# A tuned two-layer transformer kernel: VectorE's score tiles as TensorE tasks of their own, small PV bursts, and four elementwise steps on GpSimd

## The chip, the cores and the metric

The kernel runs on one core of a Trainium2 chip. The metric is the device time of one execution in microseconds (us), lower is better. All times here are of fast executions of one core, unless a line says otherwise. With one core there is no second die to compare with, so an execution counts as slow when it is more than 1.5% above the fastest of the same kernel.

## The reference

Four residual blocks over one sequence of 2048 tokens with 512 features: attention, feed-forward, attention, feed-forward.

```python
def _A_ref(x, wqkv, wo):                       # 32 heads of 16
    qkv = (x @ wqkv).reshape(B, S, 3, 32, 16)  # then transposed
    scores = einsum("bhqd,bhkd->bhqk", q, k) * 16 ** -0.5
    o = einsum("bhqk,bhkd->bhqd", softmax(scores), v)
    return o.transpose(0, 2, 1, 3).reshape(B, S, D) @ wo
def _B_ref(x, w1, b1, w2, b2):                 # 512 -> 1376 -> 512
    h = gelu(einsum("bsd,df->bsf", layernorm(x), w1) + b1)
    return einsum("bsf,fd->bsd", h, w2) + b2
x = x + _A_ref(layernorm(x), A_wqkv, A_wo);  x = x + _B_ref(layernorm(x), ...)
x = x + _A_ref(layernorm(x), A_wqkv, A_wo);  x = x + _B_ref(layernorm(x), ...)
```

The scores of both attention layers are 2 x 32 x 2048 x 2048 numbers, which is 4096 tiles of 128x512. Every one needs an exponential.

## The kernel before

The program is laid out when it is built. A list scheduler keeps a clock of its own, gives every instruction a planned duration, and emits for each engine a fixed order. **The plan is not used when the kernel runs, but the order it led to is.** In the tuple of an instruction, the number after the reads and writes is the planned duration in us.

```python
class Sched:                                   # [cut]
    def best(self, e):                         # what engine e takes next
        f = self.P.free[e]
        lim = f + self.LOOK[e]
        for t in self.pend[e]:
            r = self.task_ready(t)             # by planned durations
            if r <= lim: ...                   # ready: the lowest (prio, seq)
            else: ...                          # else: the one ready first
```

Score tiles go two ways. ScalarE takes two or three tiles at a time through its exponential. VectorE takes single tiles: an integer add on the fp32 score gives the bits of an approximate bf16 exponential, three more integer adds give shifted copies, and TensorE multiplies all four with V and three scaled copies of V, so that the errors average out. The matmuls of exponentials with V are called PV; several of them in a row are a burst. The work between two transfers of an attention accumulator out of PSUM (TensorE's output memory) is a segment; there are 88. GpSimd makes the scaled copies of V (`vs`).

```python
            dts = []                           # VectorE's tiles that ride along
            while self.wide and len(grp) + len(dts) < 4:
                d = self.take_d([rows already used in this run])   # [cut]
                if d is None: break
                dts.append(d)
            ops = []
            for (sg, j), b in zip(grp, banks):
                ops.append(self.score(sg, j, b))
            for sg, j, b, bt, w in dts:        # one TensorE task for all of them
                ops.append(self.score(sg, j, b))
            ...
            yield Task("pe", 0.0, ops)
    # [cut] the scaled copies of V, three for each group of n key blocks
    yield Task("pool", 0.8, [I(lambda e, k=k: e.tensor_scalar(out=self.vs[:, q, k - 1, i:i + n, :], in0=src, scalar1=WSHIFT[k], scalar2=None, op0=ALU.mult),
                               [("V", hg, kb) for kb in kbs], [("vs", q, i + k2) for k2 in range(n)], 0.15 + 0.06 * n, ...) for k in (1, 2, 3)])
    # [cut] the norm apply, and at the end of a segment: division, transpose
    Task("dve", prio, [I(... e.tensor_scalar(out=dst, in0=x, scalar1=mean, scalar2=rs, op0=ALU.subtract, op1=ALU.mult), ..., 0.39)])
    yield Task("dve", 1.2, [I(... e.tensor_tensor(out=ob[:, :, 0:16], in0=T[:, :, 0:16], in1=rv..., op=ALU.mult), [RA, ("rv", a)], [("ob", o)], 0.15 + 0.26 * W / 512)])
    yield Task("dve", 1.2, [I(... e.transpose(self.OT[:, hg, 0:W], self.ob[:, o, 0:W]), [("ob", o)], [("OT", hg)], 0.17 + 0.53 * W / 512)])
```

A score matmul has 32 rows, so a head takes one of four groups of TensorE's rows (`tile_position=(32 * hp, 0)`), and a run of up to four score matmuls can use four different groups. Gaps that the plan leaves on TensorE are filled with matmuls by zeros (`zw`), which are meant to keep its clock up.

Of the kernel before, what the change touches and what calls it, by code (L numbers as in the profile page):

```python
# [14 lines left out]
ALU = mybir.AluOpType  # L15
# [417 lines left out]
DLANE = 5  # L433
DBATCH = 2
# [11 lines left out]
PV_LEAST = 0.75  # L446


class Builder:
# [330 lines left out]
    def ln_apply(self, tt, slot, i, dst, dres, prio):  # L780
        c = 4 * slot + i
        return Task("dve", prio, [I(lambda e: e.tensor_scalar(out=dst, in0=self.xres[:, tt, :], scalar1=self.mv[:, c, 0:1], scalar2=self.rs[:, c:c + 1], op0=ALU.subtract, op1=ALU.mult),
                                    [("x", tt), ("mv", c), ("rs", slot)], [dres], 0.39)])
# [16 lines left out]
    def job_qkv_tile(self, L, tt, slot, i, left, prio, what):  # L800
# [9 lines left out]
        yield self.ln_apply(tt, slot, i, xnr, RX, prio)  # L810
# [83 lines left out]
        if not start:  # L894
            yield Task("dve", prio, [I(lambda e: e.tensor_tensor(out=sq, in0=v4, in1=v4, op=ALU.mult), [("qk", qs, k) for k in range(k0, k1)], SR, 0.12 + 0.0085 * N)])
# [65 lines left out]
    def job_qt(self, sg, s):  # L961
        L, part, hg = sg["L"], sg["part"], sg["hg"]
        k = (L // 2) * 2 + part
        q = yield ("get", "qt")
        sg["qslot"] = q
        yield ("keys", [("scl", L, part)])
        W = sg["W"]
        src, RS = (self.psbf(self.q0bank)[:, 0:512], ("ps", self.q0bank)) if s is None else (self.qraw[:, s, 0:W], ("qraw", s))
        yield Task("dve", 0.4, [I(lambda e: e.tensor_scalar(out=self.QT[:, q, 0:W], in0=src, scalar1=self.scl[:, k, hg:hg + 1], scalar2=self.qbias[:, 0:1], op0=ALU.mult, op1=ALU.add),
                                  [RS, ("scl", k), ("qbias",)], [("qt", q)], 0.39)])  # L970
        if s is None:
            self.S_.release("mb", self.q0bank)
        else:
            self.S_.release("qraw", s)
        self.S_.mark(("qt", sg["i"]))
        if sg["dks"] and not (L == 1 and sg["nparts"] == 2 and part == 0):
            step = 1 if L == 1 and sg["qc"] == 0 else len(sg["dks"])
            for i in range(0, len(sg["dks"]), step):
                self.S_.spawn(self.job_vs(sg, i, sg["dks"][i:i + step]), 0.8)
# [66 lines left out]
    def flow_scores(self):  # L1046
# [11 lines left out]
        while True:  # L1058
# [43 lines left out]
            for sg, j, b, bt, w in dts:  # L1102
                ops.append(self.score(sg, j, b))
# [9 lines left out]
            for d in dts:  # L1113
                self.d_load(d)
# [68 lines left out]

    def close_batch(self):
        bt = self.batch
        self.batch = None
        bt["closed"] = True
        if bt["loaded"] == len(bt["tiles"]):
            self.S_.spawn(self.job_d(bt), 2.0)
# [9 lines left out]
    def d_loaded(self, bt, w, b):  # L1199
        self.dload -= 1  # L1200
        if b == DLANE:
            self.lane_busy = False
        else:
            self.S_.release("mb", b)
        self.d_ready(bt, 0, bt["unit"], [w])
# [34 lines left out]
    def try_pv(self):  # L1240
        S_ = self.S_
        while True:
# [16 lines left out]
            if value(r) < PV_LEAST and not self.starved and len(near) < sg["n"] - sg["sub"]:  # L1259
                return  # L1260
# [23 lines left out]
            S_.submit(Task("pe", 1.0, ops), cb=lambda sg=sg, pick=pick: self.pv_done(sg, pick))  # L1284

# [11 lines left out]
    def job_segend(self, sg):  # L1297
# [44 lines left out]
        yield Task("dve", 1.2, [I(lambda e: e.tensor_tensor(out=ob[:, :, 0:16], in0=T[:, :, 0:16], in1=rv.unsqueeze(2).broadcast_to([128, nb, 16]), op=ALU.mult), [RA, ("rv", a)], [("ob", o)], 0.15 + 0.26 * W / 512)])  # L1342
# [39 lines left out]
    def job_yt(self, L, tt, slot, i, left, pr):  # L1382
        S_ = self.S_
        xr = yield ("get", "xn")
        yield self.ln_apply(tt, slot, i, self.xn[:, xr, :], ("xn", xr), pr - 1)
# [140 lines left out]
    def build(self):  # L1526
# [4 lines left out]
        self.pv_first = False  # L1531
        self.starved = False
# [78 lines left out]
```

## Time and profile before

| | before |
|---|---|
| median of 4 runs | 1710.28 us (1708.60 to 1712.83) |
| span of the profiled run | 1708.6 us |
| busy: TensorE, VectorE, ScalarE, GpSimd | 93%, 80%, 94%, 22% |
| mean granted TensorE clock | 0.983 |
| exponentials on ScalarE, tiles on VectorE | 1348, 758 |

The prediction below shows the main lines of this profile. Three more views are needed later. In all lines PE is TensorE's matmuls, PEld its weight loads, DVE VectorE, ACT ScalarE, POOL GpSimd and SP SyncE. The first is from the page's costliest groups (line, engine, operation, shapes, count; busy us and mean ns; idle before it and the releaser): GpSimd's copies of V. With half of its time idle before them, they look harmless.

```profile
L986 POOL TENSOR_SCALAR vs<-V 128x340 bf16<-128x340 bf16 (+3 forms) x312 | 255.7, 826 | 859.7 <-PE ps L1278 833.1
```

The second is the page's 40 slices of the run, each digit the busy share of one slice in tenths; the last line is the granted clock.

```profile
ACT  4878999999999999999999999999999999999996
POOL 4045522102211121101212133411011101132220
PEclk9989999999999999999899999999999999999999
```

The third is the timeline: start, duration, engine, line, operation, and how many. Four score matmuls on four row groups take 0.40 us together.

```profile
508.09 0.40 PE L1127 MATMUL ps<-QT,KT 32*128 32x512 bf16 x4
```

### The profile page before, as it was taken

How to read it: one execution, taken by the hardware profiler on the slowest of the kernel's cores; microseconds unless marked ns; L12 is line 12 of the kernel's file. 1: busy time of each engine (PE TensorE's matmuls, PEld its weight loads, DVE VectorE, ACT ScalarE, POOL GpSimd, SP SyncE). 2: the span in 40 equal slices, each digit the busy share in tenths (PEclk: the TensorE clock that was granted, in tenths of full speed). 3: DMA queues.
4: the chain of work that ended last, by engine and by line, in shares of the span. 5: the costliest groups of instructions: out<-in, count | busy, mean ns of one | idle time of the engine just before them, and what ended most of it. 6: DMA issues, size and time to landing. Idle time of an engine off the chain costs nothing.

```text
span 1708.6 us, 46394 instructions
## 1 busy us (share of the span) xinstructions
PE 1585.4 (93%) x19711; PEld 568.6 (33%) x19711; DVE 1374.4 (80%) x3011; ACT 1609.6 (94%) x1426; POOL 378.5 (22%) x640
## 2 busy tenths in 40 slices
PE   8988999999999999999999998999999999999998
PEld 5222333233223223332223333323232233344444
DVE  6878998859876798768878799886888869887783
ACT  4878999999999999999999999999999999999996
POOL 4045522102211121101212133411011101132220
PEclk9989999999999999999899999999999999999999
DMA  6552000112101120112532230000000100010000
GB/s 167 104 103 69 26 12 8 47 43 59 33 17 41 40 73 14 29 28 69 117 54 54 56 87 18 17 20 11 14 8 8 20 15 5 5 21 7 19 10 14
DMA packets 181259, 66.70 MB, mean 39 GB/s; under 512 B 160859, under 2 KB 175424, under 8 KB 181056
## 3 DMA queue, kind: packets, MB, share of 16 engines
q1 hardware_dynamic: 181056, 63.75, 16.6%
q8 instruction: 158, 2.59, 0.6%
q14 instruction: 45, 0.37, 0.1%
HBM read 19.96 MB, written 15.30 MB: 21 GB/s over the span
## 4 chain that ended last, share of the span: by engine, by line
PE 47%; ACT 40%; DVE 8%; POOL 2%; issue 2%; DMA 1%; SPq 0%; DVEq 0%; POOLq 0%
ACT PT L1110 37%; PE ps L1127 15%; PE ps L1278 13%; PE ps L1035 4%; PE ps L841 4%; PE ps L1397 4%; DVE dp L1195 3%; PE ps L1364 3%; PE ps L1435 3%; ACT h L1427 2%; DVE dp L1223 2%; POOL vs L986 1%; DVE accT L1304 1%; PE ps L1038 1%; ACT L1110 1%
## 5 line engine op out<-in xcount | busy, mean ns | idle before, releaser
L1110 ACT ACTIVATE PT<-ps 128x1536 bf16<-128x1536 f32 (+1 forms) x1348 | 1534.3, 1262 | 67.0 <-PE ps L1127 61.3
L1127 PE MATMUL ps<-QT,KT 32*128 32x512 bf16 (+1 forms) x4608 | 604.2, 363 | 108.5 <-ACT PT L1110 43.8
L1195 DVE TENSOR_SCALAR dp<-ps 128x512 uint16<-128x512 f32 x758 | 510.2, 682 | 208.4 <-PE ps L1127 200.7
L1278 PE MATMUL ps<-PT,V 128*17 128x512 bf16 (+1 forms) x3751 | 469.7, 363 | 0.4 <-DVE accT L1304 0.4
L1223 DVE TENSOR_SCALAR dp<-dp 128x1024 uint16<-128x1024 uint16 (+1 forms) x1170 | 443.2, 422 | 12.7 <-PE ps L1278 8.2
L986 POOL TENSOR_SCALAR vs<-V 128x340 bf16<-128x340 bf16 (+3 forms) x312 | 255.7, 826 | 859.7 <-PE ps L1278 833.1
L1278 PE MATMUL ps<-dp,vs 128*17 128x512 bf16 (+1 forms) x2571 | 397.3, 359 | 0.0
L1127 PEld LDWEIGHTS ps<-QT,KT 32*128 32x128 bf16 x4608 | 163.4, 91 | 637.8 <-issue 173.3
L1035 PE MATMUL ps<-wqkv,zw 128*32 128x256 bf16 x6152 | 241.5, 280 | 1.1 <-DVE accT L1304 1.1
L1278 PE MATMUL ps<-dp,V 128*17 128x512 bf16 (+1 forms) x857 | 201.4, 364 | 3.0 <-DVE accT L1304 2.9
L1035 PEld LDWEIGHTS ps<-wqkv,zw 128*32 128x32 bf16 x6152 | 144.5, 97 | 93.3 <-issue 76.0
L1278 PEld LDWEIGHTS ps<-PT,V 128*17 128x17 bf16 x3751 | 114.7, 88 | 91.1 <-issue 73.7
L1278 PEld LDWEIGHTS ps<-dp,vs 128*17 128x17 bf16 x2571 | 101.9, 89 | 85.3 <-issue 71.4
L1397 PE MATMUL ps<-yT,wf 128*128 128x512 bf16 (+3 forms) x396 | 98.5, 359 | 0.5 <-DVE h L1421 0.3
L841 PE MATMUL ps<-wqkv,xnT 128*128 128x512 bf16 x336 | 94.2, 389 | 2.9 <-DVE dp L862 2.1
L1304 DVE STREAM_TRANSPOSE accT<-ps 128x512 f32<-128x512 f32 (+1 forms) x88 | 58.3, 662 | 24.4 <-PE ps L1278 22.9
L1421 DVE TENSOR_SCALAR h<-ps,b1c 128x512 bf16<-128x512 f32 (+2 forms) x88 | 62.0, 705 | 13.9 <-PE ps L1397 13.5
L1364 PE MATMUL ps<-wo,OT 128*128 128x512 bf16 x240 | 67.4, 383 | 0.2
L1278 PEld LDWEIGHTS ps<-dp,V 128*17 128x17 bf16 x857 | 48.9, 88 | 38.4 <-issue 24.3
L906 POOL TENSOR_TENSOR qt<-n,qy 128x32 f32<-128x32 f32 x32 | 11.1, 347 | 160.1 <-DVE qy L902 159.6
L1344 DVE STREAM_TRANSPOSE OT<-ob 128x512 bf16<-128x512 bf16 (+1 forms) x72 | 46.0, 640 | 0.2
L1397 PEld LDWEIGHTS ps<-yT,wf 128*128 128x128 bf16 (+1 forms) x396 | 29.5, 99 | 46.5 <-issue 18.6
(154 smaller groups left out, 820.1 us busy)
## 6 DMA issues: line engine op xcount, KB each, us to landing
wf<-in_B_w_dram SPq DMA_DIRECT2D x90, 128.0 KB, 2.8
q_scr<-qk SPq DMA_DIRECT2D x22, 256.0 KB, 2.1
k_scr<-qk SPq DMA_DIRECT2D x12, 256.0 KB, 2.0
out_dram<-xres SPq DMA_DIRECT2D x16, 128.0 KB, 1.7
v_scr<-vst SPq DMA_DIRECT2D x12, 136.0 KB, 2.0
V<-v_scr SPq DMA_DIRECT2D x8, 204.0 KB, 4.5
wqkv<-in_A_wqkv_dram SPq DMA_DIRECT2D x3, 512.0 KB, 3.9
q_scr<-h SPq DMA_DIRECT2D x6, 256.0 KB, 2.1
```

Of the source, the lines that this page charges most:

```text
L841: yield Task("pe", prio, [I(lambda e, c=c: e.matmul(self.ps[:, b, :], lhsT=xnT[:, c, :], rhs=self.wqkv[:, c, which * 512:which * 512 + 512 ...
L986: yield Task("pool", 0.8, [I(lambda e, k=k: e.tensor_scalar(out=self.vs[:, q, k - 1, i:i + n, :], in0=src, scalar1=WSHIFT[k], scalar2=None ...
L1035: P.op("pe", lambda e, p=p: e.matmul(self.ps[p:p + 32, b, 0:w], lhsT=self.zw[:, 0:32], rhs=rhs[:, 0:w], start=st, stop=st, skip_group_chec ...
L1110: S_.submit(Task("act", 1e-5 * gi, [I(lambda e, pt=pt, n=n, b0=b0: e.activation(out=self.PT[:, pt:pt + n, :], in_=self.ps[:, b0:b0 + n, :] ...
L1127: return [I(lambda e, kb=kb, i=i: e.matmul(self.ps[:, b, i * W:(i + 1) * W], lhsT=self.KT[32 * hp:32 * hp + 32, hg, kb * 128:(kb + 1) * 12 ...
L1195: self.S_.submit(Task("dve", 0.0, [I(lambda e: e.tensor_scalar(out=self.dp[:, u, w * 512:(w + 1) * 512], in0=self.ps[:, b, :], scalar1=BIT ...
L1223: yield Task("dve", pr, [I(lambda e, k=k, v=v: e.tensor_scalar(out=self.dp[:, v, 0:N], in0=self.dp[:, u, 0:N], scalar1=float(SHIFT[k]), sc ...
L1278: ops.append((i, I(lambda e, hp=hp, v=v, ap=ap[:, i * W:(i + 1) * W], first=first and i == 0, W=W: e.matmul(self.ps[32 * hp:32 * hp + 17, ...
L1304: yield Task("dve", 0.3, [I(lambda e: e.transpose(self.accT[:, a, 0:W], self.ps[:, ACCB, 0:W]), [("ps", ACCB)], [RA], 0.15 + 0.53 * W / 512)])
L1364: yield Task("pe", pr, [I(lambda e, hg=hg, i=i, b=b: e.matmul(self.ps[:, b, :], lhsT=self.OT[:, hg, i * 128:(i + 1) * 128], rhs=self.wo[:, ...
L1397: yield Task("pe", pr, [I(lambda e, c=c: e.matmul(self.ps[0:M, b, off:off + W], lhsT=self.w1(fc, c), rhs=self.yT[:, c, 0:W], start=(c == 0 ...
L1421: S_.submit(Task("dve", pr - 0.7, [I(lambda e, fc=fc, M=M, b=b: e.tensor_scalar(out=hv[0:M, fc * W:(fc + 1) * W], in0=self.ps[0:M, b, 0:W] ...
```

## The change

The intent is to give ScalarE, the bound, fewer score tiles. VectorE is to take more of them, and for that it is relieved of four kinds of work that go to the idle GpSimd. TensorE's idle time is to be used for small PV bursts instead of zeros. There are two parts.

*Scheduling*: VectorE's tiles become TensorE tasks of their own, one more is started when VectorE is about to run dry (`d_solo`), and PV bursts that are too small to be worth it are taken when TensorE would idle for 0.4 us.

*Moves*: four kinds of work go to GpSimd: norm apply, (x - mean) * rs; Q scaling, one multiply and add on Q; squares, for the norms of Q and K; and the division of a segment's output by its sum of exponentials.

```diff
+D_IDLE = 1.0
+D_PRIO = 0.5
+PV_IDLE = 0.4
     def ln_apply(self, tt, slot, i, dst, dres, prio, eng="dve"):      # called with "pool", but for the start
-        return Task("dve", prio, [I(lambda e: e.tensor_scalar(... op0=ALU.subtract, op1=ALU.mult), [...], [dres], 0.39)])
+        return Task(eng, prio, [I(lambda e: e.tensor_scalar(... op0=ALU.subtract, op1=ALU.mult), [...], [dres], 0.39 if eng == "dve" else 1.55)])
         # squares
-            yield Task("dve", prio, [I(... in0=v4, in1=v4, op=ALU.mult ..., 0.12 + 0.0085 * N)])
+            yield Task("pool", prio, [I(... in0=v4, in1=v4, op=ALU.mult ..., 0.2 + 0.035 * N)])
         # Q scaling
-        yield Task("dve", 0.4, [I(lambda e: e.tensor_scalar(out=self.QT[:, q, 0:W], ... op0=ALU.mult, op1=ALU.add), ..., 0.39)])
+        eng = "dve" if s is None or W < 512 else "pool"
+        yield Task(eng, 0.4, [I(lambda e: e.tensor_scalar(out=self.QT[:, q, 0:W], ... op0=ALU.mult, op1=ALU.add), ..., 0.39 if eng == "dve" else 1.55)])
         # scores
-            for sg, j, b, bt, w in dts:
-                ops.append(self.score(sg, j, b))
+            for d in dts:
+                S_.submit(Task("pe", -0.5, self.score(d[0], d[1], d[2])), cb=lambda d=d: self.d_load(d))
+    def d_solo(self):
+        if not self.wide or self.P.free["dve"] - S_.now + sum(pending VectorE work) > D_IDLE:
+            return
+        d = self.take_d([])
+        if d is not None:
+            S_.submit(Task("pe", D_PRIO, self.score(d[0], d[1], d[2])), cb=lambda: self.d_load(d))
         # PV
             if value(r) < PV_LEAST and not self.starved and len(near) < sg["n"] - sg["sub"]:
-                return
+                t = self.P.drain + PV_IDLE
+                if S_.now < t or self.pv_out:
+                    ...                        # look again at t
+                    return
         # division
-        yield Task("dve", 1.2, [I(... op=ALU.mult), [RA, ("rv", a)], [("ob", o)], 0.15 + 0.26 * W / 512)])
+        yield Task("pool", 0.6, [I(... op=ALU.mult), [RA, ("rv", a)], [("ob", o)], 0.2 + 0.55 * W / 512)])
```

(Cuts are marked with dots; the arithmetic of the moved instructions is unchanged.)

## The prediction

> **What bounds the kernel now.** I read the page first: busy shares, the 40 slices, the chain.
>
> ```profile
> PE 1585.4 (93%) x19711; PEld 568.6 (33%) x19711; DVE 1374.4 (80%) x3011; ACT 1609.6 (94%) x1426; POOL 378.5 (22%) x640
> ...
> PE 47%; ACT 40%; DVE 8%; POOL 2%; issue 2%; DMA 1%; SPq 0%; DVEq 0%; POOLq 0%
> ```
>
> Two engines stand at 93 and 94%, so the shares alone do not decide. The costliest groups do:
>
> ```profile
> L1110 ACT ACTIVATE PT<-ps 128x1536 bf16<-128x1536 f32 (+1 forms) x1348 | 1534.3, 1262 | 67.0 <-PE ps L1127 61.3
> L1127 PE MATMUL ps<-QT,KT 32*128 32x512 bf16 (+1 forms) x4608 | 604.2, 363 | 108.5 <-ACT PT L1110 43.8
> L1195 DVE TENSOR_SCALAR dp<-ps 128x512 uint16<-128x512 f32 x758 | 510.2, 682 | 208.4 <-PE ps L1127 200.7
> L1223 DVE TENSOR_SCALAR dp<-dp 128x1024 uint16<-128x1024 uint16 (+1 forms) x1170 | 443.2, 422 | 12.7 <-PE ps L1278 8.2
> L1035 PE MATMUL ps<-wqkv,zw 128*32 128x256 bf16 x6152 | 241.5, 280 | 1.1 <-DVE accT L1304 1.1
> ```
>
> The columns are line, engine, operation, shapes, count; then busy us and mean ns; then idle before and its releaser. 6152 of TensorE's matmuls multiply by `zw`, a tile of zeros: filler that keeps the clock up, 241.5 us in which TensorE looks busy and makes nothing. ScalarE has no filler. It waited only 67.0 us before its 1348 exponentials. The table of windows confirms it in the middle of the run (PE, PEld, DVE, ACT, POOL busy of 100 us):
>
> ```profile
> 500.00:600.00 100.00, 93.40 (x1153) 32.75 (x1153) 73.15 (x156) 97.69 (x83) 15.00 (x16) 1.00 0.19 42
> 1400.00:1500.00 100.00, 92.63 (x1430) 34.07 (x1431) 90.12 (x198) 99.40 (x88) 16.79 (x15) 1.00 0.02 5
> ```
>
> So **ScalarE is the bound** from about 32 us (first exponential) to 1686 us (last), and the kernel gets shorter by taking score tiles from it. There are 4096 tiles of 128x512; VectorE has 758 of them, ScalarE the other 3338. TensorE is a close second bound, since it runs in order and feeds both.
>
> Last, the largest single stall of ScalarE after the start, in the order of time:
>
> ```profile
> 103.72 3.95 SPq L817 DMA_TRANSPOSE xnT<-xn  x2
> ...
> 108.29 0.41 DVE L782 TENSOR_SCALAR xn<-xres,mv,rs 128x512 bf16<-128x512 bf16 x1 [7.16 <-DMA xnT<-xn]
> ...
> 109.74 1.03 PE L1127 MATMUL ps<-QT,KT 32*128 32x512 bf16 x4 [6.94 <-DVE dp L1195]
> ...
> 110.87 1.45 ACT L1110 ACTIVATE PT<-ps 128x1536 bf16<-128x1536 f32 x1 [6.23 <-PE ps L1127]
> ```
>
> A norm apply waits on VectorE for a buffer that a late DMA frees; a VectorE score tile stands behind it, TensorE behind that, ScalarE behind that: 6.23 us lost.
>
> **What the Trainium skill says.** SBUF — State Buffer, section "Who interferes with whom": VectorE in a two-port mode and GpSimd share a port pair under an exclusive lock, and the second to start is blocked. The trace agrees in direction, with less than whole blocking on average: the 1024-column integer copies of L1223 took 417 ns (902 that met no GpSimd instruction), 520 ns (83 that began during one), at most 953 ns. The PSUM reads of L1195 took 674 to 685 ns either way. GPSIMD Engine Reference, section "Key points": for elementwise work VectorE is about twice as fast. Here it is worse: 340 columns took GpSimd 1089 ns and 68 took 427, which is 2.43 ns a column, so 512 columns are about 1.51 us (my estimate) against 0.41 to 0.45 us on VectorE. TensorEngine Tiling (Array Packing), section "Key Properties": changing the tiling mode drains TensorE. The trace fits: between score matmuls (row tiles) and PV matmuls (column tiles) its weight loads show gaps of 0.23 us put down to issue, and a PV burst of 8 takes 0.60 us from start to the next scores. TensorE: Matmul & The Clock Gate, section "What's actually happening": idle TensorE falls to half clock. Here the granted clock was 0.983 on average, so what filler removal can do to it is open.
>
> **The change part by part.** The schedule is made when the program is built, so I counted the instructions of both built programs; only counts are used, no planned times.
>
> 1. *More tiles on VectorE.* 852 instead of 758, so ScalarE has 94 fewer. Its exponentials fall from 1348 to 1310. One costs 1534.3 / 1348 = 1.138 us of engine time (the means of 1262 overlap), so 38 x 1.138 = **43 us off the bound**. The gain is spread over the run: cut into 16 equal parts by score tiles, every part has fewer ScalarE tiles than before, by 1 to 15.
>
> 2. *VectorE's bill.* Removed: Q scaling 71 x 0.445 = 31 us, norm apply 70 x 0.41 = 27 (busy), squares about 21, divisions 29; together 108. Added: 94 tiles at 510.2 / 758 = 0.673, 63 us; 153 copies of 1024 columns at 0.387 (427.7 / 1104) less 24 of 512 at 0.26, 53 us. Sum +8 us. Lock: GpSimd will be busy about twice the share, so I take some 340 instead of 156 copies meeting it, at about 80 ns each: +15. VectorE comes to about 1374 + 8 + 15 = 1397 us, 84% of a shorter span. It had 334 us idle, of which 200.7 waiting for score tiles. **Not the bound.**
>
> 3. *GpSimd's bill.* Q scaling 71 x 1.51 = 107; norm apply 70 x 1.51 = 106; squares 16 of 1024 elements and 24 of 512, at an assumed 2.4 ns an element, 69; divisions 56 x 0.72 + 16 x 0.45 = 47 (like its 256-element tensor operations at 649 to 749 ns). Sum 329, so 378 + 329 = about 707 us, 42%. Most is beside the path: Q tiles have three buffers, and a segment of scores lasts some 18 us against about 6 us of GpSimd work. Only from 100 to 265 us is it dense: eight segments at about 9 us and twelve Q tiles at about 4 us, 120 of 165 us. There, late shifted V tiles could hold TensorE. I charge **5 us**, another 3 for the longer first chain from K norms to the scale (squares and Q scaling on GpSimd).
>
> 4. *The stall at 104 us.* The norm apply leaves VectorE's queue, so the copy out of PSUM behind it no longer waits: **-5 us**. In GpSimd's new order the three Q tiles of this stage stand before the norm apply that must wait for the DMA, so it should not come back there.
>
> 5. *TensorE's bill.* Each VectorE tile is multiplied with V four times instead of once: PV matmuls 7179 to 7485, +306, about 38 bursts of 8 at 0.60 = +23 us. Runs of PV rise from 755 to 863, and changes of tiling mode from 2687 to 2777: 90 x about 0.15 = +14. Filler falls from 6515 to 4456 matmuls; 2059 x (241.5 / 6152) = -81 us busy. TensorE's sum falls by some 44 us, in step with the span, so it stays at 93%: neither relief nor a new wall. Separate tasks for VectorE's scores let ScalarE's go first when a lane isn't free (PE waited 43.2 us for DVE dp L1195), but 735 score runs hold a VectorE tile against 612, more of them in front ("D before A"). I take the two as cancelling, with +3 for the noise of a tighter schedule.
>
> Sum: -43 + 8 - 5 + 3 = -37, so 1710.5 - 37 = about **1673 us**.
>
> **The rivals.** *A, TensorE in order takes it back.* Each extra VectorE tile is one more place where late VectorE work holds TensorE. For: PE waited 43.2 us in 69 such places, up to 6.9. Against: ScalarE's own waits in the steady part were only some 50 us together, in gaps of mostly 0.2 to 0.5. If they grow by half, +25: 1695 us, within 2%. *B, GpSimd becomes the bound in the dense stage* or holds Q tiles: 10 to 20 us, near 1688. For: operations over three times slower, planned as one in-order queue. Against: 42% load, deep buffers. *C, it goes better:* with VectorE's lanes decoupled, ScalarE's waits halve: another 15 to 20, about 1655. For: a TensorE filled with useful bursts instead of zeros is what the 208 us of waiting VectorE lacked. *D, the clock falls with the filler.* If it dropped to 0.95, TensorE would need about 3% more and become the bound: about 1700. The two windows above show 1.00 with fillers; PV bursts replace them, so I think little of it.
>
> **Range and chances.** The 43 us are firm as long as ScalarE stays the bound; the rest is a spread of about 15 either way, longer on the slow side because of A and B. 8 in 10: 1652 to 1697. Two per cent lies at 1676.3, just beyond my value: faster 0.57, same 0.40, slower 0.03.
>
> **What would show it.** Right: exponentials 1310 at about 1.14 us, ScalarE busy near 1566 with waits of 60 to 80 us before L1110's successor, and windows in the middle still at 97% or more; L1195's successor x852; GpSimd near 700 us with Q scaling at 1.5 us; no 6 us stall near 104 us; filler busy near 160 us; granted clock 0.97 or more. Wrong: ScalarE's waits at 100 us or more, put down to TensorE scores which in turn waited for DVE dp (A) or for POOL vs or QT (B); copies of L1223 above 500 ns on average; or a clock below 0.96 (D).

## The result, and the profile after

| | before | after |
|---|---|---|
| runs | 1710.01, 1710.54, 1712.83, 1708.60 | 1786.59, 1790.51, 1763.32, 1774.49 |
| median | 1710.28 us | 1780.54 us (mean of the three fast runs 1774.8) |
| ratio of fast runs | | 1.0376, 95% interval 1.029 to 1.0462 |
| granted clock | 0.983 (profiled run) | 0.952, 0.948, 0.969, 0.958 |

The kernel became 3.8% **slower**. It should have become 2.2% faster, and the range from 1652 to 1697 us doesn't hold the result. A ratio in this document is the mean time of one kernel's fast runs over the mean of the other's fast runs of the same rounds, so it isn't quite the ratio of the medians. The run of 1790.51 us is 1.54% above the fastest and is left out of it. The spread has also grown from 4 us to 27 us, and the longer runs are those with the lower clock.

The page of the profiled run (busy shares, slices, the chain that ended last, then groups) has these lines:

```profile
PE 1677.8 (94%) x17958; PEld 544.2 (30%) x17958; DVE 1449.3 (81%) x2981; ACT 1582.0 (89%) x1389; POOL 696.0 (39%) x893
...
ACT  4868889999999989899978999989999699898995
POOL 6879643312532243413343347531224111134320
PEclk9979999999999989999999999989999598899999
...
PE 55%; DVE 15%; ACT 13%; POOL 12%; issue 3%; DMA 2%; SPq 0%; POOLq 0%; DVEq 0%
...
L1114 ACT ACTIVATE PT<-ps 128x1024 bf16<-128x1024 f32 (+1 forms) x1311 | 1506.3, 1245 | 167.5 <-PE ps L1129 160.7
L1129 PE MATMUL ps<-QT,KT 32*128 32x512 bf16 (+1 forms) x4608 | 701.1, 370 | 62.5 <-DVE dp L1206 34.3
L1206 DVE TENSOR_SCALAR dp<-ps 128x512 uint16<-128x512 f32 x852 | 574.7, 683 | 156.1 <-PE ps L1129 149.9
L1237 DVE TENSOR_SCALAR dp<-dp 128x1024 uint16<-128x1024 uint16 x1299 | 545.9, 464 | 18.9 <-PE ps L1298 14.3
L990 POOL TENSOR_SCALAR vs<-V 128x340 bf16<-128x340 bf16 (+3 forms) x312 | 259.2, 838 | 244.8 <-PE ps L1298 223.0
L973 POOL TENSOR_SCALAR QT<-qraw,scl,qbias 128x512 bf16<-128x512 bf16 x71 | 63.3, 892 | 506.7 <-PE ps L1129 417.9
...
L785 POOL TENSOR_SCALAR xn<-xres,mv,rs 128x512 bf16<-128x512 bf16 x70 | 157.8, 2261 | 1.5
```

ScalarE tells where the time went. Its busy time fell by 27.6 us (1609.6 to 1582.0), but its wait before the exponentials rose by 100.5 us (67.0 to 167.5). ScalarE's share of the chain fell from 40% to 13%, and VectorE and GpSimd together rose from 10% to 27%. ScalarE is no longer the bound: it waits for scores, and in the stalls shown below TensorE then waits for VectorE, and VectorE for something new. The waits of VectorE name it (engine, line, waited for; us in total, times, longest):

```profile
DVE OT L1368 <- POOL ob L1366: 33.0, 32, 3.8
...
DVE rv L1361 <- POOL accT L1359: 11.2, 9, 2.9
```

`ob` is the division, which VectorE did itself before. Now VectorE stands in its fixed order at the transpose of `OT`, and the division isn't done. The timeline shows what the division itself was behind, here at 1380 us:

```profile
1380.41 3.37 POOL L990 TENSOR_SCALAR vs<-V 128x340 bf16<-128x340 bf16 x3
...
1383.74 0.62 POOL L1366 TENSOR_TENSOR ob<-accT,rv 128x256 bf16<-128x256 f32 x1
1384.40 0.71 DVE L1368 STREAM_TRANSPOSE OT<-ob 128x512 bf16<-128x512 bf16 x1 [3.79 <-POOL ob L1366]
1385.03 0.39 DVE L1237 TENSOR_SCALAR dp<-dp 128x1024 uint16<-128x1024 uint16 x1
...
1385.47 0.38 PE L1298 MATMUL ps<-dp,vs 128*17 128x512 bf16 x1 [1.64 <-DVE dp L1237]
...
1386.69 1.03 PE L1129 MATMUL ps<-QT,KT 32*128 32x512 bf16 x4
1387.40 1.45 ACT L1114 ACTIVATE PT<-ps 128x1536 bf16<-128x1536 f32 x1 [2.50 <-PE ps L1129]
```

Read it downwards. Three copies of V take 3.37 us on GpSimd; the plan gives them 3 x 0.45 = 1.35 us. So the division comes 2 us later after them than the plan has it. VectorE waits 3.79 us for it, with integer copies behind it; TensorE waits 1.64 us for one of those; ScalarE waits 2.50 us. Each engine stands at the item that is next in its fixed order, and what lies behind it waits too. Of the 32 waits for a division, 27 have three five-block copies of V directly in front of the division on GpSimd.

The last-but-one line has a second message. A run of four score matmuls takes 1.03 us there, against a median of 0.60 in this kernel and 0.40 in the kernel before: the granted clock has dropped to half. This stretch at half clock begins at 1386.6 us, at the end of the stall, and lasts 37.5 us, the longest of the run. Added up over the records of the clock, the half-clock time grew from 58 us in 10 stretches to 171 us in 18. TensorE's busy time, which was to fall by 44 us, rose by 92 us, in part because of that. Its idle time did not grow (span less busy time: 123 us before, 107 after), and its waits for VectorE's tiles before scores even fell (43.2 to 34.3 us in all). In the profile the loss thus shows more as TensorE at half clock than as TensorE idle.

### The profile page after: what moved, and what is told of

It is laid out like the page before. It is cut to its first block, busy times and chain, and to the rows that moved or that the text cites. A ratio compares the mean times of both kernels' runs of the same rounds, so it can differ in the third digit from the quotient of the medians.

```text
span 1784.8 us, 43596 instructions
## 1 busy us (share of the span) xinstructions
PE 1677.8 (94%) x17958; PEld 544.2 (30%) x17958; DVE 1449.3 (81%) x2981; ACT 1582.0 (89%) x1389; POOL 696.0 (39%) x893
## 4 chain that ended last, share of the span: by engine, by line
PE 55%; DVE 15%; ACT 13%; POOL 12%; issue 3%; DMA 2%; SPq 0%; POOLq 0%; DVEq 0%
PE ps L1129 20%; PE ps L1298 16%; ACT PT L1114 10%; DVE dp L1237 5%; POOL vs L990 5%; DVE dp L1206 5%; PE ps L1421 4%; PE ps L1039 4%; POOL xn L785 4%; PE ps L1459 3%; PE ps L1388 3%; PE ps L844 3%; ACT h L1451 1%; POOL QT L973 1%; PE ps L1042 1%
## 5 line engine op out<-in xcount | busy, mean ns | idle before, releaser
L1114 ACT ACTIVATE PT<-ps 128x1024 bf16<-128x1024 f32 (+1 forms) x1311 | 1506.3, 1245 | 167.5 <-PE ps L1129 160.7
L1129 PE MATMUL ps<-QT,KT 32*128 32x512 bf16 (+1 forms) x4608 | 701.1, 370 | 62.5 <-DVE dp L1206 34.3
L1206 DVE TENSOR_SCALAR dp<-ps 128x512 uint16<-128x512 f32 x852 | 574.7, 683 | 156.1 <-PE ps L1129 149.9
L1237 DVE TENSOR_SCALAR dp<-dp 128x1024 uint16<-128x1024 uint16 x1299 | 545.9, 464 | 18.9 <-PE ps L1298 14.3
L1298 PE MATMUL ps<-dp,vs 128*17 128x512 bf16 (+1 forms) x2877 | 445.0, 370 | 9.0 <-DVE dp L1237 8.3
L973 POOL TENSOR_SCALAR QT<-qraw,scl,qbias 128x512 bf16<-128x512 bf16 x71 | 63.3, 892 | 506.7 <-PE ps L1129 417.9
L1039 PE MATMUL ps<-wqkv,zw 128*32 128x256 bf16 x4056 | 184.9, 283 | 0.7 <-DVE accT L1328 0.6
L785 POOL TENSOR_SCALAR xn<-xres,mv,rs 128x512 bf16<-128x512 bf16 x70 | 157.8, 2261 | 1.5
L1039 PEld LDWEIGHTS ps<-wqkv,zw 128*32 128x32 bf16 x4056 | 98.8, 98 | 85.8 <-issue 67.4
L844 PE MATMUL ps<-wqkv,xnT 128*128 128x512 bf16 x336 | 98.7, 403 | 11.4 <-DMA xnT<-xn 8.2
L1366 POOL TENSOR_TENSOR ob<-accT,rv 128x256 bf16<-128x256 f32 (+1 forms) x72 | 43.2, 600 | 69.7 <-DVE rv L1361 69.4
```

The lines of the kernel that those rows point to most:

```text
L785: return Task(eng, prio, [I(lambda e: e.tensor_scalar(out=dst, in0=self.xres[:, tt, :], scalar1=self.mv[:, c, 0:1], scalar2=self.rs[:, c:c ...
L844: yield Task("pe", prio, [I(lambda e, c=c: e.matmul(self.ps[:, b, :], lhsT=xnT[:, c, :], rhs=self.wqkv[:, c, which * 512:which * 512 + 512 ...
L973: yield Task(eng, 0.4, [I(lambda e: e.tensor_scalar(out=self.QT[:, q, 0:W], in0=src, scalar1=self.scl[:, k, hg:hg + 1], scalar2=self.qbias ...
L1039: P.op("pe", lambda e, p=p: e.matmul(self.ps[p:p + 32, b, 0:w], lhsT=self.zw[:, 0:32], rhs=rhs[:, 0:w], start=st, stop=st, skip_group_chec ...
L1114: S_.submit(Task("act", 1e-5 * gi, [I(lambda e, pt=pt, n=n, b0=b0: e.activation(out=self.PT[:, pt:pt + n, :], in_=self.ps[:, b0:b0 + n, :] ...
L1129: return [I(lambda e, kb=kb, i=i: e.matmul(self.ps[:, b, i * W:(i + 1) * W], lhsT=self.KT[32 * hp:32 * hp + 32, hg, kb * 128:(kb + 1) * 12 ...
```

## The experiments

Rival theories when they were planned: **the queue** (GpSimd's moved work stands in one in-order queue and comes late); **the lock** (GpSimd's longer busy time slows VectorE's integer copies through the shared memory ports, see the prediction; their mean, over 1024 columns and a few of 512, rose from 422 to 464 ns); **the clock** (fewer zero matmuls let the clock fall); **TensorE's order** (own tasks, more bursts). "Time in the first 16 segments" below is the time up to the 16th of the 88 transfers of an attention accumulator out of PSUM in the profiled run; it holds the dense start of layer 1. All kernels gave correct results.

### First round: which part, and which theory

**e1_sched_only**: the changed kernel with the four moves undone.

```diff
-        yield self.ln_apply(tt, slot, i, xnr, RX, prio, "dve" if start else "pool")
+        yield self.ln_apply(tt, slot, i, xnr, RX, prio)
-            yield Task("pool", prio, [I(... in0=v4, in1=v4 ...
+            yield Task("dve", prio, [I(... in0=v4, in1=v4 ...
-        eng = "dve" if s is None or W < 512 else "pool"
+        eng = "dve"
-        yield Task("pool", 0.6, [I(... [("ob", o)], 0.2 + 0.55 * W / 512)])
+        yield Task("dve", 1.2, [I(... [("ob", o)], 0.15 + 0.26 * W / 512)])
```

> The changed kernel with its four moves to GpSimd undone; score tasks, solo tiles and small PV bursts stay (852 -> 824 VectorE tiles, filler 4808). Theory LOCK (GpSimd's extra work blocks VectorE's copies and makes everything behind late): the loss is gone, 1680 to 1700 us, copies back at about 0.43 us. Theory CLOCK (fewer fillers and tighter bursts let TensorE fall to half clock): filler is as scarce as in the changed kernel, so it stays near 1750 to 1780 with a clock of about 0.95. Theory PACKED (the plan leaves TensorE and VectorE no slack): about 1740 to 1780 with a clock above 0.97.

Measured: 1696.45 us, ratio 0.9925 (0.99 to 0.9951), clock 0.984. The scheduling part alone gains 0.75%. ScalarE waited 81.6 us before the exponentials. So the scheduling part did not bring the loss. (The lock's range came true, the clock's and the packed plan's did not.)

**e2_pool_only**: the kernel before with the four moves and nothing else (the same lines as above, the other way round).

> The kernel before with the four moves to GpSimd alone (758 -> 789 VectorE tiles, filler 6439, nearly as before). LOCK: most of the loss is here, 1740 to 1780 us, copies of 1024 columns at 0.47 us. CLOCK: filler is there, so 1690 to 1715 us, clock 0.98. PACKED: as before or a little better, 1695 to 1715.

Measured: 1775.03 us, ratio 1.0386 (1.0353 to 1.0418), clock 0.97. **The moves alone bring the whole loss**, while this kernel keeps most of its zero matmuls (6439, against 6515 before). Its copies took 456 ns on average, and VectorE waited 43.9 us for divisions.

**e3_fewer_fillers**: the kernel before, with the same order of everything else and a third of the zero matmuls left out.

```diff
+FILL_KEEP = 0.68
-        for i in range(n * FILL_N // w):
+        N0 = n * FILL_N // w
+        keep = max(1, int(N0 * FILL_KEEP + 0.5))
+        long = N0 / keep                       # the plan still gives them the time of all
+        for i in range(keep):
```

> The kernel before with every instruction in its place and a third of the zero matmuls left out (6515 -> 4421, as many as the changed kernel has). CLOCK: the clock falls from 0.983 to about 0.95 and the time rises to 1730 to 1770 us. LOCK and PACKED: within 5 us of before, perhaps a little faster, clock 0.97 or more.

Measured: 1711.6 us, ratio 1.0036 (0.999 to 1.0082), clock 0.977, with 4421 zero matmuls, fewer than the 4456 of the changed kernel. One run of four took 1725.87 us. In this order, the missing filler alone isn't the cause.

**e4_pool_extra**: the kernel before, the same order, and 208 scratch instructions on GpSimd after the V copies. They read and write a buffer nobody uses; half have the form of the norm apply, half that of the Q scaling.

```diff
+        for o in vs[2::3]:                     # after every third copy of V
+            after[id(o)] = [mk(lambda e: e.tensor_scalar(out=self.dumA[:, :], in0=self.dumA[:, :], ... op0=ALU.subtract, op1=ALU.mult)),
+                            mk(lambda e: e.tensor_scalar(out=self.dumA[:, :], in0=self.dumA[:, :], ... op0=ALU.mult, op1=ALU.add))]
```

> The kernel before with every instruction in its place and some 210 more GpSimd instructions on a scratch tile of 512 columns, about 300 us busy, as much as the change adds. LOCK: VectorE's 1024-column copies rise from 0.43 to about 0.47 us on average, VectorE's work runs late, 1730 to 1770 us. CLOCK and PACKED: within 10 us of before.

Measured: 1823.29 us, ratio 1.0673 (1.0649 to 1.0697), clock 0.948, from work that does nothing. The page's slices and the two scratch groups:

```profile
ACT  4945556899999999999999989889999999999996
...
POOL 4188675412333223321332235852122313345440
...
L1542 POOL TENSOR_SCALAR dumA<-dumA,dumS 128x512 bf16<-128x512 bf16 x104 | 228.9, 2201 | 0.0
...
L1543 POOL TENSOR_SCALAR dumA<-dumA,dumS 128x512 bf16<-128x512 bf16 x104 | 97.5, 938 | 10.8
```

From the third to the seventh slice ScalarE's digits are 4 to 6, just where GpSimd's are 5 to 8. The time in the first 16 segments rose from 262.5 to 356.4 us, which is 94 of the 115 us lost. VectorE's copies slowed only from 422 to 434 ns, 1170 x 12 ns = 14 us. So lateness on GpSimd costs far more than the lock does, and more than any theory expected. The clock fell to 0.948 with all the zero matmuls in place, while TensorE was idle for 229 us instead of 123: here it **follows** a starved TensorE.

### Second round: the queue or the lock

**e5_true_plan**: the changed kernel. Only planned durations of GpSimd's instructions are set to what the trace shows; the scheduler makes a new order from them.

```diff
-   ... [dres], 0.39 if eng == "dve" else 1.55)])          # norm apply
+   ... [dres], 0.39 if eng == "dve" else 2.12)])
-   ... SR, 0.2 + 0.035 * N)])                             # squares
+   ... SR, 0.18 + 0.027 * N)])
-   ... [("qt", q)], 0.39 if eng == "dve" else 1.55)])     # Q scaling
+   ... [("qt", q)], 0.39 if eng == "dve" else 0.8)])
-   ... 0.15 + 0.06 * n, ...) for k in (1, 2, 3)])         # copies of V
+   ... 0.22 + 0.17 * n, ...) for k in (1, 2, 3)])
-   ... [("ob", o)], 0.2 + 0.55 * W / 512)])               # division
+   ... [("ob", o)], 0.16 + 0.5 * W / 512)])
```

(Two small instructions of the norm statistics were corrected too.)

> The changed kernel, planned again with GpSimd's durations as its trace has them (norm apply 2.12 us instead of 1.55, Q scaling 0.8 instead of 1.55, five-tile V job 1.07 instead of 0.45). Theory QUEUE (GpSimd runs behind the plan, and engines that run in order stand behind what it is late with): most of the loss goes, 1670 to 1710 us. Theory LOCK (VectorE's copies blocked by GpSimd's port use, which no plan can mend): still 1745 to 1785 us.

Measured: 1722.2 us, ratio 1.007 (1.0039 to 1.0101), clock 0.985. Nearly the same work on the same engines (867 VectorE tiles and 1305 exponentials, against 852 and 1311), in another order, is 3.1% or 52 us faster by the ratios, give or take 16 us. That is most of the loss, though 12 us short of the range that the queue expected. GpSimd was busy 700.9 us, more than in the changed kernel, and VectorE's copies took 467 ns, as slow as there. So the lock and GpSimd's load stayed, and most of the loss went. It also has no more zero matmuls than the changed kernel (4437 against 4456), and its clock is back. Of the two waits of VectorE shown above, this is left:

```profile
DVE rv L1361 <- POOL accT L1359: 4.6, 5, 1.7
DVE OT L1368 <- POOL ob L1366: 4.0, 6, 1.1
```

**e6_norm_fma**: the changed kernel, with the norm apply on GpSimd as x * rs + (-mean * rs) instead of (x - mean) * rs, and its planned 1.55 us kept.

```diff
+        yield Task("pool", prio, [I(... out=nm, in0=mean, in1=rs, op=ALU.mult ...)])
+        yield Task("pool", prio, [I(... out=nm, in0=nm, scalar1=-1.0, scalar2=0.0, op0=ALU.mult, op1=ALU.add ...)])
+        if eng == "pool":
+            return Task(eng, prio, [I(lambda e: e.tensor_scalar(out=dst, in0=x, scalar1=rs, scalar2=nmr, op0=ALU.mult, op1=ALU.add), ..., NORM_D)])
```

> The changed kernel with the norm apply on GpSimd written as multiply and add (with two small instructions more for each group) and planned at 1.55 us as before. The trace of the extra-work run shows 0.77 us for this form against 2.08 for subtract and multiply on the same tile. QUEUE and LOCK both: better, as 70 x 1.3 = 90 us of GpSimd work go; QUEUE 1700 to 1740, LOCK 1740 to 1765 (a third of the extra GpSimd time gone, a third of the loss).

Measured: 1760.4 us, ratio 1.0278 (1.0247 to 1.0308), clock 0.966. One norm apply took 899 ns instead of 2261 (0.77 us alone), so GpSimd has 85 us less work in all. The best estimate is a help of about 1% (the intervals just overlap), and a loss of 2.8% remains. That is the lock's range; the queue had expected more.

**e7_norm_on_vector**: the changed kernel with the norm apply back on VectorE (two call sites lose their "pool").

> The changed kernel with the norm apply alone back on VectorE. QUEUE: the longest item of GpSimd's queue is gone, 1695 to 1735. LOCK: half of the added GpSimd time is gone, half of the loss: 1735 to 1750. If the norm apply is not the cause: 1760 to 1785.

Measured: 1754.85 us, ratio 1.0279 (1.0219 to 1.0339), clock 0.972. The same as e6, and between the ranges: less help than the queue or the lock expected. VectorE still waited 27.1 us for divisions. The norm apply is one contributor, not the main one: the three moves that are left lose 2.8%.

**e8_lock_steady**: the kernel before, the same order, and 168 scratch instructions (2.08 us alone, 2.28 on average), three after each five-block group of V copies. The first of them runs at 226 us, so hardly any falls in the dense start.

> The kernel before with every instruction in its place and 3 x 56 scratch instructions of 2.08 us on GpSimd, only in the stages where it was idle (350 us, more than the whole change adds). LOCK: 1750 to 1790 us. QUEUE: within 15 us of before, as nothing of the kernel stands behind them for long.

Measured: 1755.45 us, ratio 1.0267 (1.0226 to 1.0307), clock 0.972. This is the lock's range, so taken alone it speaks for the lock. The profile says otherwise, because the scratch work also stands in front of GpSimd's last sums for a segment, which VectorE waits for (before, then e8):

```profile
DVE rv L1337 <- POOL accT L1335: 7.6, 6, 2.3
...
DVE rv L1339 <- POOL accT L1337: 39.7, 11, 7.6
```

By groups of eight segments, VectorE's waits for GpSimd grew in the second, third, eighth and eleventh group (by 10.3, 6.0, 14.2 and 5.1 us), and these groups lost time (12.6, 6.5, 15.6 and 8.1 us, of 43 in all). The fourth, fifth, ninth and tenth group hold 90 of the 168 scratch instructions, and there no such wait grew. Their 1024-column copies took 458 ns instead of 426, nearly as much longer as in the changed kernel, and yet these four groups together ended 2 us sooner than in the kernel before. So e8's loss is lateness again, and where ScalarE is the bound the slower copies cost nothing that shows.

### Third round: mend it, and take the scheduling part apart

**e9_fma_true**: e5 and e6 together (true planned durations, norm apply as multiply-add planned at 0.8 us).

> The changed kernel with both mends: GpSimd's durations planned as measured, and the norm apply as multiply and add (0.8 us). 868 VectorE tiles, 1304 exponentials. QUEUE: the queue is shorter and true to plan, 1690 to 1715 us, better than the true plan alone (1722). If what is left there is not GpSimd's (PACKED): 1715 to 1730, no better.

Measured: 1712.34 us over 20 runs, ratio 1.0015 (0.9998 to 1.0033), clock 0.982. All of the loss is gone and nothing is gained, although 44 exponentials fewer are made than before (1304).

**e10_sched_no_bursts**: e1 with the small PV bursts undone (the timer is replaced by the old `return`).

> The scheduling part alone, without the small PV bursts on idle TensorE (816 VectorE tiles instead of 824, filler 5461 instead of 4808). If the bursts cost ScalarE (each is a drain of TensorE that a score group may stand behind): 1680 to 1693 us, waits of ScalarE below 70 us. If they are what brings the gain: 1698 to 1710.

Measured: 1719.78 us, ratio 1.0057 (1.0042 to 1.0072). Without the bursts e1's gain of 0.75% turns into a loss of 0.57%, worse than either range. Without the bursts there is no gain.

**e11_sched_old_groups**: e1 with VectorE's tiles in ScalarE's runs again (the old lines of the diff), and bursts and `d_solo` kept.

> The scheduling part alone, with VectorE's score tiles again inside the task of ScalarE's group (793 tiles instead of 824, 1334 exponentials). If tasks of their own are the gain: 1700 to 1712 us. If they put late tiles ahead of ScalarE's: equal to the scheduling part, 1690 to 1700, with fewer waits for the copy out of PSUM.

Measured: 1703.76 us, ratio 0.9973 (0.9958 to 0.9988). About a third of e1's gain is left, so tasks of their own matter too; the gains of the two parts don't simply add up. TensorE's scores took 624.9 us here, 681.9 in e1.

**e12_sched_true_vs**: e1 with true planned durations for V copies and norm statistics, the moves still undone.

> The scheduling part alone, planned with the true time of the shifted V copies on GpSimd (five tiles 1.07 us instead of 0.45); 824 tiles as without. QUEUE: shifted V is late in the present plan too, so 1680 to 1692 us. If the old mismatch is harmless because nothing stands behind it: 1692 to 1700 as without.

Measured: 1707.11 us, ratio 0.999 (0.9975 to 1.0004). **Correcting the V copies' planned time gains nothing here, and even loses 0.65% against e1; in the changed kernel it is worth some 27 us (e17, below).** So the wrong number did no harm while little that was urgent stood behind a copy of V: without the moves VectorE waited 7.6 us (kernel before) and 0.6 us (e1) for the sums `accT` of GpSimd, and for no division.

### Fourth round: TensorE's row groups, and the moves one by one

In e1 and in the changed kernel a run of four score matmuls takes longer than before. The form of 512 columns took 530.4 us in the kernel before and 595.1 in e1, at the same clock:

```profile
L1127 PE MATMUL ps<-QT,KT 32*128 32x512 bf16 x3584 | 530.4, 389 | 97.9 <-ACT PT L1110 39.3 <-DVE dp L1195 38.5 <-DVE QT L969 2.8
```

```profile
L1129 PE MATMUL ps<-QT,KT 32*128 32x512 bf16 x3584 | 595.1, 386 | 49.7 <-ACT PT L1114 19.6 <-DVE dp L1206 15.5 <-DVE mv L773 2.3
```

The built programs show why. As a task of its own, a VectorE tile often lands beside a score matmul of the same row group: 468 score matmuls follow directly on one of the same row group in the changed kernel and 445 in e1, against 123 before (in each count some are the two halves of one tile). Two matmuls on one row group follow each other instead of running side by side. In the changed kernel's timeline:

```profile
511.02 0.60 PE L1129 MATMUL ps<-QT,KT 32*128 32x512 bf16 x4
```

The median run of four is 0.60 us there and in e1, 0.40 before and in e11.

**e13_sched_rows**: e1, with the tile chosen only when the task is issued, from the row group that has been free longest.

```diff
+            if t.late is not None:
+                t.ops = t.late()
-                S_.submit(Task("pe", -0.5, self.score(d[0], d[1], d[2])), cb=lambda d=d: self.d_load(d))
+                S_.submit(self.d_task(-0.5, d), cb=lambda d=d: self.d_load(d))
+    def d_row(self, d):                        # [cut]
+        best = min([j] + [k for k in sg["todod"] if ok(k)], key=cost)
```

> The scheduling part alone, with VectorE's tile put on a free row group when it is issued (repeats 445 -> 199; 828 VectorE tiles). Theory ROWS (colliding row groups cost TensorE 0.2 us a run): runs of four back at 0.40 us, TensorE's score time back from 680 to about 615 us, 1675 to 1690 us. If the collisions lie in TensorE's slack: 1692 to 1705 as the scheduling part.

Measured: 1697.72 us, ratio 0.9932 (0.9908 to 0.9956). The mechanism is confirmed: 199 such neighbours, runs of four back at 0.40 us, the 512-column form at 538.3 us.

```profile
507.70 0.40 PE L1133 MATMUL ps<-QT,KT 32*128 32x512 bf16 x4
```

The expected gain did not come: this is e1's time. The scores take TensorE 65 us less (681.9 to 616.9) and the kernel ends no sooner; the idle time before them grew (53.8 to 79.5 us), and more zeros were multiplied (5516 matmuls against 4808). The second expectation came true: in e1 the collisions lie in TensorE's slack.

**e14_mended_rows**: e9 and e13 together.

> The changed kernel with true GpSimd durations, norm apply as multiply and add, and free row groups (repeats 464 -> 202; 861 VectorE tiles, 1307 exponentials). ROWS: 1675 to 1695 us. Otherwise 1705 to 1720 as without.

Measured: 1698.0 us, ratio 0.9942 (0.9919 to 0.9964), clock 0.991. Here choosing the row late is worth 14 us over e9 (1712.34 us), between the two expectations.

**e15_changed_rows**: the changed kernel with e13's rows and nothing else.

> The changed kernel with free row groups alone (repeats 468 -> 196; 873 VectorE tiles). ROWS says 15 to 25 us better than the changed kernel, 1755 to 1765, with the GpSimd queue still in the way; if TensorE was only late because GpSimd was, no change: 1775 to 1785.

Measured: 1759.7 us, ratio 1.0304 (1.0277 to 1.0332), clock 0.964. The best estimate is 12 us better than the changed kernel, in the range that the rows theory had set, but the intervals overlap. VectorE still waited 32.1 us for divisions. Most of the loss isn't TensorE's.

**e16_cheap_moves_rows**: rows, true planned durations, and only Q scaling and divisions on GpSimd; norm apply and squares stay on VectorE.

> True GpSimd durations, free row groups, and only Q scaling and divisions on GpSimd (0.77 and 0.62 us each), norm apply and squares on VectorE; 847 VectorE tiles, 1313 exponentials. QUEUE and ROWS together: the best of all, 1665 to 1685 us. If VectorE's port lock and the longer chains eat the rest: 1690 to 1710.

Measured: 1691.71 us (1688.5 to 1692.42), ratio 0.9894 (0.9875 to 0.9913), clock 0.984. The fastest median of all, 1.06% under the kernel before and with a narrow spread, though in the second range and not in the one that was hoped for. The page:

```profile
L1118 ACT ACTIVATE PT<-ps 128x1024 bf16<-128x1024 f32 (+1 forms) x1313 | 1497.5, 1254 | 82.7 <-PE ps L1133 78.0
...
L1258 DVE TENSOR_SCALAR dp<-dp 128x1024 uint16<-128x1024 uint16 (+1 forms) x1290 | 521.9, 446 | 22.7 <-PE ps L1319 18.6
```

The exponentials take 36.8 us less than in the kernel before, and ScalarE waits 15.7 us more for them; the difference, 21 us, is close to the gain (18.6 us between the two profiled spans).

### Fifth round: which planned duration

**e17_true_vs_only**: the changed kernel, with the planned duration of the V copies corrected and nothing else.

```diff
-   ... 0.15 + 0.06 * n, ...) for k in (1, 2, 3)])
+   ... 0.22 + 0.17 * n, ...) for k in (1, 2, 3)])
```

> The changed kernel with the planned time of the shifted V copies alone corrected; norm apply still planned at 1.55 us. If the V copies are what makes the queue late: 1720 to 1740 us, near the fully true plan (1722). If the norm apply is: 1765 to 1785, as the changed kernel.

Measured: 1741.13 us, ratio 1.0217 (1.0149 to 1.0285), clock 0.978. One line of the plan, for an instruction that the change doesn't touch, is worth 1.6% or 27 us of the 52 by the ratios, give or take 19 us: the two intervals (1.029 to 1.0462 for the changed kernel) just don't overlap. VectorE's wait for divisions fell from 33.0 us to this:

```profile
DVE OT L1368 <- POOL ob L1366: 1.8, 4, 0.7
```

**e18_divisions_rows**: e16 with Q scaling back on VectorE, so that only the divisions move.

> True durations, free row groups, only the divisions on GpSimd (72 of about 0.6 us); 823 VectorE tiles, 1322 exponentials against 847 and 1313 with Q scaling there too (1692 us). If ScalarE's count decides: 1695 to 1705. If the port lock decides: 1680 to 1692.

Measured: 1693.94 us, ratio 0.9904 (0.9876 to 0.9932). Not to be told from e16, and between the two ranges. Moving the Q scaling is worth little either way.

### Taken together

Each column is one profiled execution; the last row is the ratio of the timed runs.

| us | before | after | e2 moves only | e17 V copies planned true | e5 all planned true | e9 and multiply-add |
|---|---|---|---|---|---|---|
| first 16 segments | 262.5 | 280.6 | 271.1 | 260.6 | 268.7 | 260.4 |
| the rest | 1446.1 | 1504.2 | 1502.0 | 1472.0 | 1450.8 | 1445.9 |
| VectorE waits for divisions | none moved | 33.0 | 43.9 | 1.8 | 4.0 | 2.7 |
| one integer copy (1024 columns, a few of 512), mean ns | 422 | 464 | 456 | 469 | 467 | 460 |
| ratio | 1 | 1.0376 | 1.0386 | 1.0217 | 1.007 | 1.0015 |

The fourth row stays where it is while the ratio falls to 1, so the slower copies don't decide. The third row shrinks as soon as the V copies are planned truly; what e17 still loses goes for the larger part when the other durations are corrected too (e5), though not through the waits for divisions, which were already short. A caution: each changed duration makes a new order for the whole run, and e12 shows that a new order alone can move the time by 0.65%. The 3.1% of e5 are well beyond that; the 1.6% of e17 less so, and there the wait that went with it is the stronger sign. Most of the loss lies in the rest of the run, 58 of 76 us, not in the dense start. In the one profiled execution of the changed kernel, 26 us of it came in the ninth group of eight segments, the one with the stall at 1384 us and 58 us of half clock; e2, e15 and e17 differ from the kernel before by -2 to +4 us there. So a part of the profiled 76 us belongs to that execution, and such events make up the spread of 27 us between runs.

## Why the prediction was wrong

*Part 1, more tiles on VectorE.* The counts were right: 852 tiles and 1311 exponentials (1310 predicted). The worth was not quite: the exponentials' busy time fell by 28 us instead of 43, since one took 1.149 us instead of 1.138. Single exponentials even got shorter (1536 columns: 1486 to 1468 ns); but after a wait an exponential has no neighbour to overlap with, and the sum of all durations exceeded the busy time by 125 us instead of 167. In e1 the mean was 1.140. "43 us off the bound" also needed ScalarE to stay the bound, which it did not.

*Part 2, VectorE's bill.* The prediction allowed the lock 15 us: 340 instead of 156 copies meeting GpSimd, at 80 ns each. The 1024-column copies took 468 ns instead of 429, 1257 x 39 ns = 49 us, since 427 copies began during a GpSimd instruction and lost 150 ns each. So the term was less than a third of its size. (Its "520 ns (83 that began during one)" is not what a recount gives: 156 copies at 500 ns, which are the numbers that its sum used.) That was affordable: e5 and e9 have the same slow copies and lose 0.7% and 0.15%.

*Part 3, GpSimd's bill: this is the step that failed.* The total was right, 696 us against "about 707 us, 42%", though by luck: the norm apply took 2.26 us instead of 1.51, and the Q scaling 0.89 instead of 1.51. What failed is "Most is beside the path" and the charge of 5 and 3 us. It was worked out from load and from the number of buffers. In its place, VectorE waited 33.0 us for divisions, 32 times, and ScalarE's waits grew by 100.5 us. GpSimd takes its queue in order, and the order came from a plan that gave the five-block V copies 0.45 us each where they take 1.10 on average, and the norm apply 1.55 where it takes 2.26. With true numbers in the plan and nothing else changed, the time falls by some 52 us (e5), about half of them by the V copies (e17); with the cheaper form of the norm apply as well it is back at the kernel before (e9). The V copies' duration was in the profile of before (340 columns at 1089 ns, quoted in the prediction), and the planned one in the code. The two were never put side by side, though both were at hand.

*Part 4, the stall at 104 us.* Only half right. The stall of 6.23 us is gone, but two of 5.0 and 4.6 us stand at 99 and 106 us. The first two groups of eight segments together became 18 us longer.

*Part 5, TensorE's bill.* "TensorE's sum falls by some 44 us" was wrong in sign: +92 us. A part is the half clock: TensorE was busy at half clock for 166 us instead of 54, and if work takes twice as long there, that is some 56 us of the 92 (an estimate). A part is a term that was missing: own tasks put score matmuls on the row group of their neighbour, 65 us of busy time in e1 at the same clock. Choosing the row late brings it back to 538 us (e13). Its worth in time is unclear: nothing in e13, 14 us in e14, and 12 us, not certain, in e15.

*The rivals.* B was named, with a value of 10 to 20 us and as a matter of load in the dense stage. The mechanism was near the truth, and the size was not: 58 of the 76 us were lost outside that stage. Of its signs, waits above 100 us came true, but TensorE waited only 1.5 us for a Q tile of GpSimd and never noticeably for a copy of V, the two places that B names: GpSimd held TensorE through VectorE, a path that was not listed. D's sign came true too, a clock below 0.96 in three of the four runs. As a cause D fell: e2 loses as much with nearly all of the filler, e3 loses nothing clear with less of it, and e5 has as little filler as the changed kernel and a clock of 0.985. In e4 the clock fell because TensorE was starved. That in the changed kernel a stall starts a stretch at half clock, which then makes the loss longer, is seen at 1386 us and is likely for the rest, but not shown.

*What stays open.* The versions that gain most (e1, e13, e14, e16, e18) make 26 to 41 fewer exponentials, 30 to 47 us at 1.14 us, and gain 10 to 18 us. In e16 TensorE has 54% of the chain and ScalarE 28%, and VectorE is busy 86% of the time, so the bound has become a shared one. Which of TensorE's order and VectorE's load takes the rest isn't settled. The profiles show one place to look: the sixth group of eight segments, in the middle of the run, took 11 to 23 us longer than in the kernel before in 12 of the 15 kernels with the scheduling part (4 to 5 us in e14, e15 and e16), and 1 to 4 us longer in the four without it. In e1 and e10 ScalarE's longest single waits there are 6.3 and 11.4 us; in the kernel before the longest is 1.7.

## What to carry to other kernels

When work moves to a queue that was nearly idle, compare the planned and the traced duration of everything that is **already** in it: an error that cost nothing while nothing waited behind it becomes a stall of three other in-order engines. Load (39% busy) did not show this; the wait of the next engine for the moved result did, though not all of it (e17). And before an operation is moved, time its exact form: here one form of the same arithmetic took 0.77 us and the other 2.07.

## What the Trainium skill lacked or had wrong

- GPSIMD Engine Reference, section 4.1 (engine selection), says that one-input operations are roughly at line rate on GpSimd. Two forms of one instruction differed here: `tensor_scalar` with subtract then multiply on 128x512 bf16 took 2.07 us at least and 2.26 on average, with multiply then add 0.77 and 0.90. VectorE took 0.41 to 0.45 us for either. No page that was read has this difference.
- SBUF — State Buffer, section "Who interferes with whom", says that the second to start is blocked. Of the changed kernel's 1024-column copies, those that met no GpSimd instruction took 417 ns; 427 began during one and took 568 ns on average, at most 2.11 us, so the direction is right. But 186 of the 427 took less than 435 ns, and 146 of these ended before the GpSimd instruction did: over two fifths weren't delayed at all, so the block isn't always a full one.
- TensorEngine Tiling (Array Packing), section "Key Properties", says that different tiles run in parallel. It lacks the price of using the same tile twice running: a run of four score matmuls took 0.60 us with a repeated row group and 0.40 us without.
- No page that was read tells how much filler a kernel needs for its clock. Here a third of it could go (6515 to 4421 zero matmuls) with a clock of 0.977 after 0.983.
